# Sliding-window ALiBi attention in front of a gated feed-forward layer: q and k by head pair, a score table added on TensorE, and batch 1 inside the first group

## The chip, the cores and the metric

The kernel runs on one core of one Trainium2 chip. The metric is the device time of one launch in microseconds (us). Five engines work side by side and wait for each other by semaphores: TensorE (PE in the profile; its weight loads are PEld), VectorE (DVE), ScalarE (ACT), GpSimd (POOL) and SyncE (SP). Each runs its own instructions in order. Data lie in HBM, in SBUF (128 partitions) and, for what TensorE writes, in PSUM, which has eight banks of 128 partitions x 512 float32. 16 DMA engines carry the transfers, which SP, ACT and POOL issue.

## The reference

Eight batches of eight heads, 576 tokens, head size 64. Each token attends to itself and the 127 before it; ALiBi subtracts a slope times the distance. The attention output (4608 tokens x 512) goes through two matrices with a gate between them.

```python
scores = scale * np.matmul(q, k.transpose(0, 1, 3, 2))        # q, k, v: 8 x 8 x 576 x 64, float32
rel = pos[:, None] - pos[None, :]
slopes = 2.0 ** (-8.0 * (np.arange(H) + 1) / H)
bias = slopes[:, None, None] * (-np.abs(rel))[None, :, :]
mask = (rel >= 0) & (rel < 128)
scores = np.where(mask, scores + bias[None], -1e9)
attn = softmax(scores)                                        # written out in the reference
x = np.matmul(attn, v).transpose(0, 2, 1, 3).reshape(4608, 512)
h = x @ w_in                                                  # 512 x 2048
g = h * (1.0 / (1.0 + np.exp(-beta * h)))                     # beta: 2048
out = g @ w_out                                               # 2048 x 512
```

## The kernel before

All matrix work is in bfloat16. A batch has five token blocks (`sb`, `kb`, `qb`: four of 128 rows, one of 64) and four head pairs `p`. The steps are these; the names are those of the code and of the profile.

- `load_qk` and `load_v` (L91, L101): SP loads a block of all heads, 128 tokens x 8 heads x 64, in pieces of 256 B (one token of one head), into a float32 tile `fst` (16 buffers), and POOL casts it to bfloat16: q and k into `bst` (L96, L97), v into `vs` (L104), which has a column of ones for the softmax sum.
- `T(b, sb)` (L165): eight TensorE transposes of 128 x 128 into one PSUM tile `tps`, and one VectorE copy into `qkT` (L176), which holds q and k with the head size on the partitions.
- `SC(b, m, p)` (L184): the scores of one head pair, transposed (keys on partitions), for key blocks 0 and 1 (`m` = 0, four matmuls) or 2, 4 and 3 (`m` = 1, six matmuls), into one tile `sps` of two banks, of which there is one buffer. Four ScalarE `Exp` (L207) write `pt`; their `bias` is slope x (key position - a constant), so that ALiBi's query part drops out in the softmax. VectorE multiplies `pt` by a 0/1 mask (L211). The masks are built on POOL before the loop (L120).
- `PV(b, qb, g)` (L219): for four heads, four or eight matmuls with `pt` as weights into `pv`, then reciprocal and product on VectorE into `xn` (L238, L239).
- `X(b, qb)` (L244): four transposes of `xn` and a VectorE copy into `XT` (L254), the feed-forward input with features on partitions.
- `HS(g, j)` (L261): for token group `g` (nine of 512) and one of 16 blocks of the hidden size, four matmuls into `hps` (two banks), ScalarE `Tanh` into `sig` (L272), VectorE `(sig + 1) * hps` into `gT` (L273). Half the gate's argument and the factor 0.5 at the end turn `Tanh` into the sigmoid.
- `OS(g, i, n)` (L277): four of the 16 matmuls that make 128 output rows in `ops` (two banks); after the fourth quarter ScalarE scales them (L289) and SP stores them (L291).

`tps`, `pv` and `xt` share two PSUM buffers (`psum_t`). TensorE's order is written out by hand. A list `att` holds the attention steps of all batches, with `T` and `SC` of one half of a batch merged with `PV` and `X` of the half before. First as much of `att` runs as group 0 needs. Then, in group `g`, 16 `HS(g, j)` alternate with the 16 `OS(g - 1, ...)` and the share of `att` that the next group needs is spread between them; group 0 has only `HS`, and group 1 has its 16 `OS` two by two in its second half. Loads are issued from inside `att` half a batch ahead (`loads_ahead`, L335); the four quarters of W1 are queued on POOL behind the fourth V cast of batch 0 and those of W2 behind a V cast of batch 1.

Of the kernel before, what the change touches and what calls it, by code (L numbers as in the profile page):

```python
# [18 lines left out]
def kernel(  # L19
# [17 lines left out]
    NP = H // 2  # L37
    NQB = 5
# [10 lines left out]
    REF = 63.5  # L49

    const = ctx.enter_context(tc.tile_pool(name="const", bufs=1))
    ident = const.tile([P, P], BF16, name="ident")
    identf = const.tile([NFF, NFF], F32, name="identf")
    bflat = const.tile([NFF, P], F32, name="bflat")
    beta_h = const.tile([P, NFF], F32, name="beta_h")
    one = const.tile([P, 1], BF16, name="one")
    masks = [const.tile([P, 2, 512], BF16, name=f"mask{m}") for m in range(2)]
# [3 lines left out]
    QK = [const.tile([P, 2, NP, NQB * P], BF16, name=f"qkT{i}") for i in range(2)]  # L61
    XT = const.tile([P, NDM, XTR], BF16, name="XT")
# [4 lines left out]
    fst_pool = ctx.enter_context(tc.tile_pool(name="fst", bufs=16))  # L67
    bst_pool = ctx.enter_context(tc.tile_pool(name="bst", bufs=4))
    pt_pool = ctx.enter_context(tc.tile_pool(name="ptp", bufs=11))
    xn_pool = ctx.enter_context(tc.tile_pool(name="xn", bufs=2))  # L70
# [3 lines left out]
    psum_h = ctx.enter_context(tc.tile_pool(name="psum_h", bufs=2, space=bass.MemoryType.PSUM))  # L74
    psum_o = ctx.enter_context(tc.tile_pool(name="psum_o", bufs=2, space=bass.MemoryType.PSUM))
# [4 lines left out]
    def load_rows(src, b, sb):  # L80
        rows = ROWS[sb]
        f = fst_pool.tile([P, H, D], F32, name="fst", tag="fst")
        nc.sync.dma_start(  # L83
            out=f[0:rows],
            in_=src[b, :, P * sb : P * sb + rows, :].rearrange("h p d -> p h d"),
        )
        return f

    staged = {}

    def load_qk(b, sb):  # L91
        rows = ROWS[sb]
        fq = load_rows(q, b, sb)
        fk = load_rows(k, b, sb)
        t = bst_pool.tile([P, 2, H, D], BF16, name="bst", tag="bst")
        nc.gpsimd.tensor_copy(out=t[0:rows, 0], in_=fq[0:rows])  # L96
        c = nc.gpsimd.tensor_copy(out=t[0:rows, 1], in_=fk[0:rows])  # L97
        staged[b, sb] = t
        return c

    def load_v(b, sb):  # L101
        rows = ROWS[sb]
        f = load_rows(v, b, sb)
        return nc.gpsimd.tensor_copy(out=VS[b % 2][0:rows, sb, :, 0:D], in_=f[0:rows])  # L104

    make_identity(nc, ident[:])
    nc.sync.dma_start(out=bflat[:], in_=moe_beta.rearrange("(j p) -> j p", p=P))
    make_identity(nc, identf[:])
    nc.vector.memset(one[:], 1.0)
# [3 lines left out]
    )  # L113

    low = dict(compare_op=ALU.is_ge, fill=0.0, base=0, channel_multiplier=-1)
    up = dict(compare_op=ALU.is_ge, fill=0.0, base=-1, channel_multiplier=1)

    def fill(m, at, n, w, sign, how):
        for e in range(2):
            nc.gpsimd.affine_select(  # L120
                out=masks[m][:, e, at : at + n * w].rearrange("p (n w) -> p n w", w=w),
                in_=bass.AP(tensor=one.tensor, offset=one[:].offset,
                            ap=[list(one[:].ap[0]), [0, n], [0, w]]),
                pattern=[[0, n], [sign, w]], **how,
            )


    fill(0, 0, 2, P, 1, low)
    fill(0, 256, 2, P, -1, up)

    fill(1, 0, 1, P, 1, low)
    fill(1, 128, 1, 64, 1, low)
    fill(1, 192, 1, P, 1, low)
    fill(1, 320, 1, 64, -1, up)
    fill(1, 384, 1, P, -1, up)
    for h in range(H):
        for half in range(2):
            nc.vector.tensor_scalar(
                out=bias[:, half, h : h + 1], in0=kpos[:], scalar1=-(REF + half * P),
                scalar2=slopes[h], op0=ALU.add, op1=ALU.mult,  # L140
            )
    for i in range(2):
        nc.vector.memset(VS[i][64:P, 4, :, :], 0.0)
        nc.vector.memset(VS[i][:, :, :, D : D + 1], 1.0)
        nc.vector.memset(QK[i][:, :, :, S:], 0.0)
    for sb in range(3):
        load_qk(0, sb)

# [9 lines left out]
    bps = psum_t.tile([P, NFF], F32, name="bps", tag="t")  # L158
    nc.tensor.transpose(out=bps[:], in_=bflat[:], identity=identf[:])
    nc.vector.tensor_scalar_mul(beta_h[:], bps[:], 0.5)  # L160
# [4 lines left out]
    def T(b, sb):  # L165
        rows = ROWS[sb]
        src = staged.pop((b, sb))
        tps = psum_t.tile([P, 2, NP, P], BF16, name="tps", tag="t")
        for i in range(2):
            for p in range(NP):  # L170
                nc.tensor.transpose(  # L171
                    out=tps[:, i, p, :],
                    in_=src[:, i, 2 * p : 2 * p + 2, :].rearrange("r h d -> r (h d)"),
                    identity=ident[:],
                )
        nc.vector.tensor_copy(  # L176
            out=QK[b % 2][:, :, :, P * sb : P * sb + rows], in_=tps[:, :, :, 0:rows]
        )

# [4 lines left out]
    def SC(b, m, p):  # L184
        qk = QK[b % 2]
        sps = psum_s.tile([P, 2, 512], F32, name="sps", tag="sps")
        for kb in ((0, 1), (2, 4, 3))[m]:
            at, after = COLS[kb]
            nq = {3: P + 64, 4: 64}.get(kb, 2 * P)
            for e in range(2):  # L190
                o = sps[:, e, at : at + min(nq, 512 - at)]
                if kb in (0, 2):
# [8 lines left out]
                    start=True, stop=True, skip_group_check=True,  # L201
                )
        pt = pt_pool.tile([P, 2, 512], BF16, name="pt", tag="pt")
        for e in range(2):
            h = 2 * p + e
            for half, cols in ((0, slice(0, OWN[m])), (1, slice(OWN[m], 512))):
                nc.scalar.activation(  # L207
                    out=pt[:, e, cols], in_=sps[:, e, cols], func=ACTF.Exp,
                    scale=qscale, bias=bias[:, half, h : h + 1],
                )  # L210
        nc.vector.tensor_tensor(out=pt[:], in0=pt[:], in1=masks[m][:], op=ALU.mult)  # L211
# [7 lines left out]
    def PV(b, qb, g):  # L219
# [19 lines left out]
        nc.vector.tensor_tensor(  # L239
# [4 lines left out]
    def X(b, qb):  # L244
# [9 lines left out]
        nc.vector.tensor_copy(out=XT[:, :, tok0 : tok0 + n1], in_=xt[:, :, 0:n1])  # L254
# [6 lines left out]
    def HS(g, j):  # L261
# [3 lines left out]
        hps = psum_h.tile([P, TOKG], F32, name="hps", tag="hps")  # L265
# [28 lines left out]
    def pvx(b, qbs):  # L294
        r = []
        for qb in qbs:
            r += [(None, lambda g=g, qb=qb: PV(b, qb, g)) for g in range(2)]
            if qb != qbs[0]:
                r.append(((b, qb - 1), lambda qb=qb: X(b, qb - 1)))
        r.append(((b, qbs[-1]), lambda: X(b, qbs[-1])))  # L300
        return r

# [10 lines left out]


    att, before = [], []
    for b in range(B):
        for m in range(2):
            a = [(None, lambda b=b, sb=sb: T(b, sb)) for sb in ((0, 1, 2), (3, 4))[m]]
            a += [(None, lambda b=b, m=m, p=p: SC(b, m, p)) for p in range(NP)]
            att.append((None, lambda b=b, m=m: loads_ahead(b, m)))  # L320
            att += merged(a, before)
            before = pvx(b, ((0, 1), (2, 3, 4))[m])
            if b == 0 and m == 1:
                att += before[:6]
                before = before[6:]
# [3 lines left out]
    def place_of(tok):  # L329
        b, s = divmod(tok - 1, S)  # L330
        return place[b, s // P]
# [3 lines left out]
    def loads_ahead(b, m):  # L335
        if m == 0:
            if b:
                for sb in (3, 4):
                    load_qk(b, sb)
                for sb in (2, 3, 4):  # L340
                    load_v(b, sb)
        elif b + 1 < B:
            for sb in range(3):
                load_qk(b + 1, sb)
            for sb in range(2):
                c = load_v(b + 1, sb)
            if b == 0:
                with tc.issue_after(c.ins):
                    for n in range(4):
                        load_w2(n)  # L350

    with tc.manual_schedule(engines={mybir.EngineType.PE}):
        for sb in range(2):
            load_v(0, sb)
        for sb in (3, 4):
            load_qk(0, sb)
        for sb in (2, 3, 4):
            c = load_v(0, sb)
            if sb == 3:
                with tc.issue_after(c.ins):  # L360
                    for n in range(4):
                        load_w1(n)
        done = 0
        while done < need[0]:
            att[done][1]()
            done += 1
        for g in range(NTG):
            items = []
            for j in range(NFF):
                items.append(lambda g=g, j=j: HS(g, j))  # L370

                lag = [2 * j - NFF, 2 * j - NFF + 1] if g == 1 else [j] if g else []
                items += [lambda g=g, n=n: OS(g - 1, n // 4, n % 4) for n in lag if n >= 0]
            target = need[g + 1] if g + 1 < NTG else len(att)
            start, span_ = done, len(items) - 3
            for n, it in enumerate(items):
                it()
                while done < min(target, start + (target - start) * (n + 1) // span_):
                    att[done][1]()
                    done += 1  # L380
# [32 lines left out]
```

The softmax here doesn't subtract the row's maximum and nothing guards it: scores larger than these inputs give would overflow.

## Time and profile before

| | |
|---|---|
| device time, median of 3 runs | 374.97 us (373.36 to 377.29) |
| the profiled execution's own time | 376.31 us |
| its span, first to last instruction | 374.6 us |
| TensorE matmul busy | 338.5 us, 90% |
| VectorE busy | 224.2 us, 60% |
| ScalarE busy | 214.4 us, 57% |
| POOL busy | 84.4 us, 23% |
| moved by DMA | 42.40 MB, mean 113 GB/s |

Durations come from one execution, by the hardware profiler; the span runs from its first to its last instruction. Busy time of TensorE counts a matmul from its issue to a modelled end, so that matmuls in a row overlap: four of 512 columns that start every 0.216 us are shown as one piece of 1.03 us. In a line of the timeline, x4 is the number of instructions in the piece, and the bracket gives the idle time of the engine ahead of it and the instruction that ended it. In a group's line the numbers behind the first bar are the busy us and the mean ns of one, those behind the second the idle time just before them and what ended most of it.

### The profile page before, as it was taken

The numbers are of one execution on the slowest core, as the hardware profiler recorded it, in microseconds if no ns is written. First come the engines' busy times: TensorE is split into PE (matmuls) and PEld (weight loads), VectorE is DVE, ScalarE is ACT, GpSimd is POOL, SyncE is SP. The second block draws the span as 40 slices with busy tenths as digits, with TensorE's granted clock in tenths as the row PEclk, the third lists the DMA queues.
The fourth block names the chain that finished last, engine by engine and source line by source line (L and its number), as shares of the span: only waits on it lengthen the run. The fifth ranks groups of instructions, "written<-read, shape, count | busy, mean of one in ns | idle before, by whom it ended". The sixth has DMA issues, their size and how long they took to land.

```text
span 374.6 us, 6713 instructions
## 1 busy us (share of the span) xinstructions
PE 338.5 (90%) x2529; PEld 172.7 (46%) x2529; DVE 224.2 (60%) x473; ACT 214.4 (57%) x437; POOL 84.4 (23%) x151
## 2 busy tenths in 40 slices
PE   2367687788999999999999999999999999999995
PEld 1145334434454455445454545454545445544442
DVE  3266467777665677665666776776767755533400
ACT  1453359375745875585846694668566854445421
POOL 7570703453122213112033303320100000000000
PEclk9999999899999999999999999999999999999999
DMA  9999999999297898954138440000000010001012
GB/s 166 209 206 202 193 195 214 192 216 180 76 214 159 159 186 170 205 126 107 50 96 187 109 104 31 28 30 29 30 28 30 30 57 29 29 29 58 28 56 86
DMA packets 121985, 42.40 MB, mean 113 GB/s; under 512 B 113232, under 2 KB 117344, under 8 KB 121952
## 3 DMA queue, kind: packets, MB, share of 16 engines
q1 hardware_dynamic: 117728, 37.77, 47.9%
q0 software_dynamic: 4224, 4.19, 6.7%
q8 instruction: 20, 0.33, 0.4%
q14 instruction: 13, 0.11, 0.1%
HBM read 36.71 MB, written 9.44 MB: 123 GB/s over the span
## 4 chain that ended last, share of the span: by engine, by line
PE 80%; DMA 6%; DVE 4%; ACT 4%; SPq 4%; issue 1%; POOL 0%; ACTq 0%
PE ops L283 34%; PE hps L267 32%; PE sps L197 4%; DMA fst<-in_k_dram 4%; PE tps L171 4%; SPq L83 4%; ACT pt L207 3%; PE xt L249 2%; PE pv L233 2%; DVE gT L273 2%; PE pv L229 2%; DMA fst<-in_v_dram 1%; ACT sig L272 1%; DVE pt L211 1%; DVE qkT L176 1%
## 5 line engine op out<-in xcount | busy, mean ns | idle before, releaser
L272 ACT ACTIVATE sig<-hps,beta_h 128x512 bf16<-128x512 f32 x144 | 99.5, 692 | 98.4 <-PE hps L267 87.4
L267 PE MATMUL hps<-XT,W 128*128 128x512 bf16 x576 | 150.7, 385 | 3.6 <-DVE gT L273 3.0
L283 PE MATMUL ops<-W,gT 128*128 128x512 bf16 x576 | 144.9, 379 | 0.0
L273 DVE SCALAR_TENSOR_TENSOR gT<-sig,hps 128x512 bf16<-128x512 bf16 x144 | 98.3, 683 | 53.0 <-ACT sig L272 52.4
L207 ACT ACTIVATE pt<-sps,bias 128x256 bf16<-128x256 f32 (+2 forms) x256 | 100.4, 480 | 34.9 <-PE sps L197 34.6
L267 PEld LDWEIGHTS <-W 128*128 128x128 bf16 x576 | 51.1, 98 | 56.5 <-issue 10.9
L283 PEld LDWEIGHTS <-gT 128*128 128x128 bf16 x576 | 51.3, 98 | 52.2 <-issue 1.7
L211 DVE TENSOR_TENSOR pt<-pt,mask 128x1024 bf16<-128x1024 bf16 x64 | 46.1, 720 | 21.2 <-ACT pt L207 20.0
L96 POOL CAST bst<-fst 128x512 bf16<-128x512 f32 (+1 forms) x40 | 24.6, 615 | 108.8 <-issue 78.7
L197 PE MATMUL sps<-qkT 64*128 64x256 bf16 (+2 forms) x320 | 28.3, 271 | 14.1 <-ACT pt L207 13.1
L104 POOL CAST vs<-fst 128x512 bf16<-128x512 f32 (+1 forms) x40 | 26.1, 659 | 65.0 <-PE pv L233 38.1
L176 DVE COPY qkT<-tps 128x1024 bf16<-128x1024 bf16 (+1 forms) x40 | 25.5, 637 | 21.5 <-PE tps L171 21.3
L171 PE MATMUL tps<-ident,bst 128*128 128x128 bf16 x320 | 28.8, 240 | 7.8 <-POOL bst L96 4.3
L239 DVE TENSOR_TENSOR xn<-pv,zs 128x256 bf16<-128x256 f32 (+1 forms) x80 | 33.7, 422 | 2.6
L289 ACT ACTIVATE osb<-ops 128x512 f32<-128x512 f32 x36 | 21.6, 601 | 20.8 <-PE ops L283 20.8
L233 PE MATMUL pv<-vs,pt 128*128 128x65 bf16 x320 | 31.0, 200 | 2.5 <-DVE xn L239 1.5
L171 PEld LDWEIGHTS <-bst 128*128 128x128 bf16 x320 | 23.5, 107 | 17.3 <-POOL bst L96 4.9
L197 PEld LDWEIGHTS <-qkT 64*128 64x128 bf16 x320 | 12.4, 97 | 38.2 <-issue 35.1
L233 PEld LDWEIGHTS <-pt 128*128 128x128 bf16 x320 | 23.6, 102 | 13.7 <-issue 1.8
L97 POOL CAST bst<-fst 128x512 bf16<-128x512 f32 (+1 forms) x40 | 25.3, 634 | 9.3 <-DMA fst<-in_k_dram 9.2
L229 PE MATMUL pv<-vs,pt 128*128 128x65 bf16 x256 | 25.8, 200 | 1.8 <-DVE qkT L176 1.2
L229 PEld LDWEIGHTS <-pt 128*128 128x128 bf16 x256 | 21.3, 102 | 8.3 <-DVE xn L239 1.3
(26 smaller groups left out, 74.3 us busy)
## 6 DMA issues: line engine op xcount, KB each, us to landing
out_dram<-osb SPq DMA_DIRECT2D x36, 256.0 KB, 2.0
fst<-in_q_dram SPq DMA_DIRECT2D x32, 256.0 KB, 4.8
fst<-in_k_dram SPq DMA_DIRECT2D x32, 256.0 KB, 4.8
fst<-in_v_dram SPq DMA_DIRECT2D x32, 256.0 KB, 5.0
W<-in_moe_w_in_dram POOLq DMA_DIRECT2D x4, 512.0 KB, 11.5
W<-in_moe_w_out_dram POOLq DMA_DIRECT2D x4, 512.0 KB, 12.6
fst<-in_q_dram SPq DMA_DIRECT2D x8, 128.0 KB, 4.2
fst<-in_k_dram SPq DMA_DIRECT2D x8, 128.0 KB, 4.2
```

The lines of the kernel that those rows point to most:

```text
L171: nc.tensor.transpose(out=tps[:, i, p, :], in_=src[:, i, 2 * p : 2 * p + 2, :].rearrange("r h d -> r (h d)"), identity=ident[:],)
L176: nc.vector.tensor_copy(out=QK[b % 2][:, :, :, P * sb : P * sb + rows], in_=tps[:, :, :, 0:rows])
L197: nc.tensor.matmul(o, lhsT=qk[64 * e : 64 * e + 64, 1, p, P * kb : P * kb + P], rhs=qk[64 * e : 64 * e + 64, 0, p, P * kb : P * kb + nq], ...
L207: nc.scalar.activation(out=pt[:, e, cols], in_=sps[:, e, cols], func=ACTF.Exp, scale=qscale, bias=bias[:, half, h : h + 1],)
L211: nc.vector.tensor_tensor(out=pt[:], in0=pt[:], in1=masks[m][:], op=ALU.mult)
L229: nc.tensor.matmul(pv[:, hl, 0 : D + 1], lhsT=weights(b, qb - 1, h, 1), rhs=vs[:, qb - 1, h, 0 : D + 1], start=True, stop=False,)
L233: nc.tensor.matmul(pv[:, hl, 0 : D + 1], lhsT=weights(b, qb, h, 0), rhs=vs[:, qb, h, 0 : D + 1], start=qb == 0, stop=True,)
L239: nc.vector.tensor_tensor(out=xn[0:nq, 4 * g : 4 * g + 4, :], in0=pv[0:nq, :, 0:D], in1=zs[0:nq].broadcast_to([nq, 4, D]), op=ALU.mult,)
L267: nc.tensor.matmul(hps[:], lhsT=W1[:, c, bass.ts(j, P)], rhs=XT[:, c, c0 : c0 + TOKG], start=(c == 0), stop=(c == NDM - 1),)
L272: nc.scalar.activation(out=sig[:], in_=hps[:], func=ACTF.Tanh, scale=beta_h[:, j : j + 1])
L273: nc.vector.scalar_tensor_tensor(out=gts[g][:, j, :], in0=sig[:], scalar=1.0, in1=hps[:], op0=ALU.add, op1=ALU.mult)
L283: nc.tensor.matmul(ops_[:], lhsT=gT[:, j, i * P : i * P + P], rhs=W2[:, j, :], start=(j == 0), stop=(j == NFF - 1),)
```

## The change

- `load_qk(b, p)` now loads one head pair: partition `r` gets tokens 4r to 4r + 3 of both heads (512 tokens), so a piece in HBM is four tokens of one head, 1 KB. POOL's cast reorders to (token in four, head, feature). The last 64 tokens of all heads come in two more loads with the first pair, into `tails`. `T(b, p, i)` makes five transposes (four of the 128 rows, one of the tail) for q or k of one pair, and two VectorE copies; the first interleaves the four.
- In batches 0 and 1 (`NPE` = 2) two matmuls per `SC` first put a table into `sps`: a diagonal matrix of slope / scale times a 128 x 512 table of key position - constant, with -1e12 where the mask is 0. The score matmuls add to it, one `Exp` covers all 1024 columns, and neither bias nor mask product follows. From batch 2 on bias and mask are as before, with the mask held once for both heads of a pair. The table comes from an iota on POOL and about 20 VectorE instructions; mask and bias tiles are made after batch 0's attention.
- All of batch 0's attention now runs ahead of group 0, its `SC` with two more `sps` buffers in the four banks that `hps` and `ops` get afterwards. `XT` of batch 0 is copied by ScalarE.
- Group 0 has `hps` on four banks (the `ops` banks too), and batch 1's `T` and `SC` come in four lumps after each four `HS`; its `PV` and `X` (but for the last `X`) follow the 16th. Group 1 runs its 16 `HS` first and its 16 `OS` after them, with `att` from the ninth `HS` on. From batch 2 on the halves of a batch are head pairs 0, 1 and 2, 3, and `PV` of a half goes over all five blocks.
- All loads of batch 1 are issued at the start, behind those of batch 0. `bflat` is issued by ScalarE. Pools: `fst` 7, `fqk` 8, `bst` 8, `xn` 6 buffers.

```diff
+    def load_qk(b, p):
+        for i, src in enumerate((q, k)):
+            f = fqk_pool.tile([P, 2, LA, D], F32, name="fqk", tag="fqk")
+            nc.sync.dma_start(
+                out=f[:].rearrange("r h a d -> r h (a d)"),
+                in_=src[b, 2 * p : 2 * p + 2, 0:LM].rearrange("h (r a) d -> r h (a d)", a=LA),
+            )
+            t = bst_pool.tile([P, LA, 2, D], BF16, name="bst", tag="bst")
+            nc.gpsimd.tensor_copy(out=t[:], in_=f[:].rearrange("r h a d -> r a h d"))
+            staged[b, p, i] = t
+        if p == 0:
...
+                nc.gpsimd.tensor_copy(out=tails[b % 2][0 : S - LM, i], in_=f[0 : S - LM])
...
+    def T(b, p, i):
+        src = staged.pop((b, p, i))
+        tps = psum_t.tile([P, LA + 1, P], BF16, name="tps", tag="t")
+        for a in range(LA):
+            nc.tensor.transpose(
+                out=tps[:, a, :], in_=src[:, a, :, :].rearrange("r h d -> r (h d)"),
+                identity=ident[:],
+            )
...
+        nc.vector.tensor_copy(
+            out=to[:, 0:LM].rearrange("c (r a) -> c r a", a=LA),
+            in_=tps[:, 0:LA, :].rearrange("c a r -> c r a"),
+        )
+        nc.vector.tensor_copy(out=to[:, LM:S], in_=tps[:, LA, 0 : S - LM])
...
-    def SC(b, m, p):
+    def SC(b, m, p, pool=None):
         qk = QK[b % 2]
-        sps = psum_s.tile([P, 2, 512], F32, name="sps", tag="sps")
+        sps = (pool or psum_s).tile([P, 2, 512], F32, name="sps", tag="sps")
+        if b < NPE:
+            for e in range(2):
+                nc.tensor.matmul(
+                    sps[:, e, :], lhsT=sident[:, 2 * p + e, :], rhs=table[m][:],
+                    start=True, stop=False, skip_group_check=True,
+                )
...
-                    start=True, stop=True, skip_group_check=True,
+                    start=b >= NPE, stop=True, skip_group_check=True,
...
+        if b < NPE:
+            nc.scalar.activation(out=pt[:], in_=sps[:], func=ACTF.Exp, scale=qscale)
+        else:
...
-        nc.vector.tensor_copy(out=XT[:, :, tok0 : tok0 + n1], in_=xt[:, :, 0:n1])
+        copy = nc.vector.tensor_copy if b else nc.scalar.copy
+        copy(out=XT[:, :, tok0 : tok0 + n1], in_=xt[:, :, 0:n1])
...
-        hps = psum_h.tile([P, TOKG], F32, name="hps", tag="hps")
+        pool, tag = (psum_o, "ops") if g == 0 and j % 2 else (psum_h, "hps")
+        hps = pool.tile([P, TOKG], F32, name="hps", tag=tag)
...
+    for b in range(1, B):
+        for half in range(2):
+            a = []
+            for p in (2 * half, 2 * half + 1):
+                a += [(None, lambda b=b, p=p, i=i: T(b, p, i)) for i in range(2)]
+                if p % 2 and b > 1:
+                    a += [(None, lambda b=b, p=p, m=m: SC(b, m, p - 1)) for m in range(2)]
+                if p % 2 or b == 1:
+                    a += [(None, lambda b=b, p=p, m=m: SC(b, m, p)) for m in range(2)]
+            if b > 1 or half:
+                att.append((None, lambda b=b, half=half: loads_ahead(b, half)))
+            att += merged(a, before)
...
+        with tc.tile_pool(name="psum_x", bufs=2, space=bass.MemoryType.PSUM) as psum_x:
+            nsc = 0
+            for p in range(NP + 1):
+                if p < NP:
+                    for i in range(2):
+                        T(0, p, i)
+                if p:
+                    for m in range(2):
+                        SC(0, m, p - 1, psum_s if nsc % 3 == 2 else psum_x)
+                        nsc += 1
...
+        for qb in range(NQB):
+            for g in range(2):
+                c = PV(0, qb, g)
+            if qb:
+                X(0, qb - 1)
+        X(0, NQB - 1)
+        with tc.issue_after(c.ins):
+            late_consts()
...
-                lag = [2 * j - NFF, 2 * j - NFF + 1] if g == 1 else [j] if g else []
-                items += [lambda g=g, n=n: OS(g - 1, n // 4, n % 4) for n in lag if n >= 0]
+                if g > 1:
+                    items.append(lambda g=g, j=j: OS(g - 1, j // 4, j % 4))
+            if g == 1:
+                items += [lambda j=j: OS(0, j // 4, j % 4) for j in range(NFF)]
             target = need[g + 1] if g + 1 < NTG else len(att)
-            start, span_ = done, len(items) - 3
+            lead = 8 if g == 1 else 0
+            start, span_ = done, len(items) - 3 - lead
             for n, it in enumerate(items):
                 it()
-                while done < min(target, start + (target - start) * (n + 1) // span_):
+                to = start + (target - start) * (n + 1 - lead) // span_
+                if g == 0:
+
+                    to = NB1 * ((n + 1) // 4) // 4 if n + 1 < NFF else target
+                while done < min(target, to):
                     att[done][1]()
                     done += 1
```

## The prediction

> **What bounds the kernel now.** I read the page's 40 slices first, then TensorE's timeline of the first 95 us, then the groups by line with shapes kept apart, then the waits.
>
> ```profile
> PE   2367687788999999999999999999999999999995
> DMA  9999999999297898954138440000000010001012
> ```
>
> From slice 11 on (94 us) TensorE is busy without a break; before that it is not, and the DMA engines are. To see what a full TensorE is worth I priced its work by its own timeline: four `hps` or `ops` matmuls take 0.864 us from start to start (groups in a row start at 224.46, 225.32, 226.19), the `sps` group of one `SC` 0.33, a 128-column transpose 0.056, a `pv` matmul 0.031, the four of `X` 0.225. The first `ops` matmul starts at 93.71. In the compiled order 119 `hps` groups, 144 `ops` groups, 44 `SC`, 200 transposes of `T`, 424 `pv` matmuls and 30 `X` follow: 272.8 us. They end at 370.8, 277.1 us later: only 4.3 us are lost there. Ahead of 93.71 stand 41.9 us of the same work, so 52 us are lost, all in the first quarter. What waits are they?
>
> ```profile
> 14.83 0.61 PE L197 MATMUL sps<-qkT 64*128 64x256 bf16 x4 [1.66 <-ACT pt L207]
> ...
> 42.44 1.87 PE L267 MATMUL hps<-XT,W 128*128 128x512 bf16 x4 [0.52 <-DVE XT L254]
> ...
> 80.19 1.89 PE L267 MATMUL hps<-XT,W 128*128 128x512 bf16 x8 [0.73 <-DVE gT L273]
> ```
>
> The columns are start, length, engine, line, and in brackets the idle time ahead with what ended it. The first line: one `sps` tile, so the next `SC` waits for four `Exp`. The second: the first `hps` starts at 42.44, and its four matmuls run at half pace. The third: `hps` groups in a row, on two banks, wait for `Tanh` and `gT`; two of them then cost 2.52 us (80.19 to 82.71) and not 1.73.
>
> ```profile
> L272 ACT ACTIVATE sig<-hps,beta_h 128x512 bf16<-128x512 f32 x144 | 99.5, 692 | 98.4 <-PE hps L267 87.4 <-DVE xn L239 10.2 <-DVE gT L273 0.3
> L273 DVE SCALAR_TENSOR_TENSOR gT<-sig,hps 128x512 bf16<-128x512 bf16 x144 | 98.3, 683 | 53.0 <-ACT sig L272 52.4
> L207 ACT ACTIVATE pt<-sps,bias 128x256 bf16<-128x256 f32 x128 | 50.2, 478 | 26.8 <-PE sps L197 26.6
> L239 DVE TENSOR_TENSOR xn<-pv,zs 128x256 bf16<-128x256 f32 x64 | 27.1, 424 | 2.1
> L176 DVE COPY qkT<-tps 128x1024 bf16<-128x1024 bf16 x32 | 22.1, 690 | 19.6 <-PE tps L171 19.5
> L176 DVE COPY qkT<-tps 128x512 bf16<-128x512 bf16 x8 | 3.4, 424 | 1.9 <-PE tps L171 1.8
> ```
>
> Here the second number after the bar is the mean ns of one. They price the new operations below.
>
> So the end is: start of the first `ops` matmul + work left on TensorE + stalls + 3.8 us (last `osb` and its store, 370.8 to 374.6). In the changed order 32 `hps` groups, not 25, and four `SC` of batch 2 stand ahead of the first `ops`; 267.5 us of priced work stand behind it. The change draws level if its first `ops` starts at 93.71 + 272.8 - 267.5 = 99.0 with no new stall behind it.
>
> **Part A, loads and batch 0, up to the first `hps`.** A 256 KB load in 256 B pieces takes 1.2 us (the casts that wait for one follow at 7.11, 8.31, 9.53). A 1 KB piece is not in this trace. Bounds: 1.2 us, and 0.68 us, since the 2 KB rows of the stores move 27 GB/s at a DMA share of 0.07 (240 to 260 us). By time per piece (18.7 and 85 ns) 1 KB lies at 47 ns: I take 0.75 us. SP issues its first load at about 0.85 and not 1.26, as `bflat` goes to ScalarE's queue; data flow from about 3.1. Eight loads of 0.75 and two tails of 0.6 land by 10.3, five loads of V by 15.7 (W1, queued on POOL behind the fourth V cast, is issued at 16 and not 20.46; its chunks took 11.5 us to land). POOL's 3.75 us of mask building go; about 3 us of iota and memsets take their place and end as q lands. VectorE's table building (about 20 instructions of 0.1 to 0.2 us) ends near 6, as the first transposes do. Both are hidden by the loads.
>
> The exponential over 1024 columns is new too. `Exp` of 256 costs 478 ns, the 512 columns of `Tanh` 692: 0.84 ns a column, hence 1.1 us, against four in 1.57. Ends: 1.0 and 1.57. Eight of them behind the first `sps` (about 10 us) and behind TensorE at half pace give the last at 20.6; the 16 table matmuls lie in this wait. Then `PV` and `X` alternate on two `psum_t` buffers: 15 tiles. One `pv` tile costs TensorE 0.44 at half pace and 0.2 drain, VectorE 0.63 (0.21 to the `xn`, 0.42 of it); two buffers make 0.69 a tile, 10.4 us, from 19.0 on. `X` copied by ScalarE (0.69) fits the same step. First `hps`: **29.3**, 13 us earlier; 27 if TensorE runs at full pace, 32 if the loads stay at 1.2.
>
> **Part B, group 0 with batch 1 in it.** The order puts four `hps`, then `T`, `T`, `SC`, `SC` of one pair, with nothing in between. A block at full pace: 3.46 for `hps` (four banks, no wait), 0.56 for ten transposes, 0.43 for the first table matmuls. The copies stand on VectorE behind three `gT` and with a fourth between them. A copy that reads 512 columns in four interleaved runs is not in the trace: 0.42 as the contiguous form, or 0.69 at the 1.03 ns a column that `gT` and `xn` pay. `xn` also reads in pieces and is nearest: 0.69, and 0.19 for the tail copy. Then `SC` can start at 6.4, its `Exp` ends at 8.0, and the second `SC`, on the one `sps` tile, at 8.8. First block 11 (half pace at its start), second 8.9. The third ends after its first `SC` at 6.7; four `hps` (10.2), the second `SC`, `T`, `T` and the two `SC` of the last pair follow by 15.8, and then 10 `PV` tiles and four `X` alone, 8.3 us plus the copy: 24.3. Sum 44.2 for 25.2 us of work; group 1 starts at **73.5** (before: 81.05). Ends: 38 with copies of 0.42 and no half pace, 48 with half pace after each wait.
>
> A rule bears on the copy. The Trainium skill, "VectorE: DVE Perf Modes", section "What auto-detection actually checks", ties the packed rate of 16-bit data to a step of one element in every tensor. The interleaved read steps 128, so the page says 0.69 and speaks against this part; without it each block would be some 0.5 us shorter. The second is on pace: `hps` at 42.44 took 1.87 and at 93.71 1.02. "TensorE: Matmul & The Clock Gate", section "What's actually happening", gives half rate after an idle window of some 3.4 us; by it the waits of 2.0 and 1.3 us in a block keep full pace.
>
> **Part C, group 1 up to `ops`.** Nine `hps` in a row at 1.265 are 11.4 us. Three more with 25 transposes and `X` reach 15.4. Then four `SC` stand between four `hps`: ScalarE needs 1.57 + 0.6 for each pair, and the one `sps` tile makes TensorE follow: 9.2. With 1.3 for half pace after the `PV` stretch: 25.9, and the first `ops` at **99.4**. Ends 22 and 28. For a check, the pace of before from its first `hps` to its first `ops` (32.2 us of work in 51.3) makes 42.4 us of work 67.5: 96.8.
>
> **Part D, behind it.** Before, two `SC` never stand closer than two `hps`/`ops` groups there. In the changed order nine pairs have one group between them (three in group 1, six later). From `SC` to `SC` the single tile needs 0.45 + 1.57 + 0.05 and up to 0.6 for a `Tanh` ahead; TensorE has 1.19 to 1.44 us to do. Stall 0.6 to 1.5, I take 0.95: 8.5 us. The eight copies of a batch cost VectorE 7.0 us and not 3.2; it was busy 14 us in 20 and goes to 16, hidden while `gT` keeps within its 1.7 us of slack (an `hps` returns to its bank after 4.2 us, its chain takes 2.5); without cover each late `gT` is a TensorE stall. The mask read twice from one tile keeps 0.72, at most 1.2; `PV` comes three groups later. Loads keep their number and have half a batch, 20 us, of lead; smaller pools cost nothing.
>
> **Sum.** 99.4 + 267.5 + 4.3 + 8.5 + 3.8 = 383.5; with 96.8, 380.9. I take 382 against a span of 374.6 (that execution took 376.3; the median shown is 375.0, 0.4 above the span, inside its spread).
>
> **Rivals.** *Slower, 378.7 to 391* (0.50): the sum; against it, that it adds up many waits, any of which may overlap. *Faster, about 369* (0.24): group 0 packs better than 44. It decides there: ScalarE has 18.4 us of work in group 0 (16 x 0.6, 8 x 1.1) and TensorE 25.2, so no engine forces 44. At 80% of TensorE group 0 takes 31.5, and the end is 369 to 370; level with before at 37, faster by over 1% below 33. Against: queues run in order. *No change, 371.2 to 378.7* (0.22): the short `SC` gaps cost nothing, since `Exp` may start earlier: 382 - 8.5 = 373.5. *Far slower, 392 or more* (0.04): late `gT`, 0.2 us for each of 112, +22; VectorE's reserve speaks against it. That the loads do not speed up costs 3 us and lies inside the first.
>
> The bounds of the terms give 366.7 (27 + 38 + 22, short gaps at half) to 395; 367 to 392 holds eight in ten, the likeliest alone 379 to 391. About 1% is what a measurement here tells from no change: faster 0.24, within 0.22, slower 0.54.
>
> **What would show it.** First `hps` at 27 to 32; group 1 at 68 to 77; first `ops` at 95 to 101; qkT copies of 0.69 and `Exp` of 1.1; TensorE waiting for `pt` 0.6 to 1.5 us about nine times behind 100 us. A group 0 under 37 us, or no such stalls, makes it wrong.

## The result: 3.8% slower

| | before | after |
|---|---|---|
| device time, median of 4 runs | 375.76 us (373.36 to 377.29) | 389.75 us (388.17 to 391.25) |
| ratio to before, 95% interval | | 1.0378 (1.030 to 1.0455) |
| span of the profiled execution | 374.6 us | 388.7 us |
| first `hps` matmul | 42.44 us | 28.68 us |
| first `hps` of group 1 | 81.05 us | 74.51 us |
| first `ops` matmul | 93.71 us | 102.76 us |

The slices of the changed kernel's page, 9.7 us each (busy tenths of TensorE, and the clock that it was granted):

```profile
PE   2987787886879998999999989998999899999996
PEclk9968897599899999999999999999999999999999
```

Two things differ from before. The broken stretch reaches to the end of slice 12 (117 us) and not of slice 10 (94 us), and in it the granted clock falls in slices 3, 4, 5, 7, 8 and 11. Behind it slices 16, 24, 28 and 32 are an 8, where before all were 9. The clock row, and every mean clock below, counts the time ahead of a trace's first clock record as full pace. That record comes at 12.5 us in the changed kernel. In the kernel before it comes at 50.5 us, and the matmuls up to there show half pace (four `hps` matmuls took 1.87 us at 42.44 and 1.89 at 47.08).

The groups by line, with shapes kept apart, hold the new operations (the second number behind the bar is the mean ns of one):

```profile
L198 DVE COPY qkT<-tps 128x512 bf16<-128x512 bf16 x64 | 43.9, 686 | 11.7 <-PE tps L192 11.3
L202 DVE COPY qkT<-tps 128x64 bf16<-128x64 bf16 x64 | 11.7, 183 | 0.0
L235 ACT ACTIVATE pt<-sps 128x1024 bf16<-128x1024 f32 x16 | 16.0, 1026 | 22.9 <-PE sps L227 22.8
L240 ACT ACTIVATE pt<-sps,bias 128x256 bf16<-128x256 f32 x96 | 37.7, 480 | 7.7 <-PE sps L227 7.4
```

The interleaved copy costs 0.69 us where 512 contiguous columns cost 0.42, and one `Exp` over 1024 columns 1.03 us where four took 1.57. Now TensorE's own timeline, a line of each kind of wait:

```profile
36.94 0.39 PE L227 MATMUL sps<-qkT 64*128 64x256 bf16 x4 [1.54 <-DVE qkT L198]
38.45 0.59 PE L213 MATMUL sps<-table,sident 128*128 128x512 bf16 x2 [1.12 <-ACT pt L235]
...
48.46 4.40 PE L306 MATMUL hps<-XT,W 128*128 128x512 bf16 x16
...
79.29 2.13 PE L306 MATMUL hps<-XT,W 128*128 128x512 bf16 x8 [0.39 <-DVE gT L312]
...
188.06 0.40 PE L227 MATMUL sps<-qkT 64*128 64x256 bf16 x6 [0.69 <-ACT pt L240]
...
226.56 0.40 PE L227 MATMUL sps<-qkT 64*128 64x256 bf16 x6 [0.94 <-ACT pt L240]
...
265.93 0.40 PE L227 MATMUL sps<-qkT 64*128 64x256 bf16 x6 [0.95 <-ACT pt L240]
...
307.15 0.40 PE L227 MATMUL sps<-qkT 64*128 64x256 bf16 x6 [1.07 <-ACT pt L240]
```

The first two are one lump of group 0: `SC` waits for the copies of the `T` just ahead of it, and the second `SC` for the `Exp` of the first. At 48.46 sixteen `hps` matmuls take 4.40 us where 3.63 is the full pace (sixteen at 55.72). At 79.29 groups of `hps` in a row wait for `gT`. The last four are short gaps between `SC`, from four batches. The waits of TensorE from 102.7 us to the end (us in all, times, longest; the kernel before has no such wait behind its first `ops`):

```profile
PE sps L227 <- ACT pt L240: 6.8, 9, 1.1
```

**Where the 14.1 us of span come from.** The first `ops` comes 9.05 us later, but with 5.3 us more of priced work done (272.8 less 267.5): 3.8 us are lost ahead of it. From there to the last `osb` 282.2 us pass for 267.5 of work, 14.7 lost; before, 277.2 for 272.8, 4.4 lost. So 10.3 us come behind the first `ops`. The 3.8 us ahead of it are a difference: the first `hps` comes 13.8 us earlier than before, and groups 0 and 1 lose that again and more.

### The profile page after: what moved, and what is told of

Read it like the earlier page. It is cut to its first block, busy times and chain, and to the rows that moved or that the text cites. A ratio compares the mean times of both kernels' runs of the same rounds, so it can differ in the third digit from the quotient of the medians.

```text
span 388.7 us, 6816 instructions
## 1 busy us (share of the span) xinstructions
PE 346.2 (89%) x2515; PEld 174.1 (45%) x2561; DVE 240.9 (62%) x560; ACT 209.9 (54%) x394; POOL 82.5 (21%) x140
## 4 chain that ended last, share of the span: by engine, by line
PE 76%; ACT 10%; DVE 9%; issue 2%; POOL 1%; POOLq 0%; ACTq 0%
PE hps L306 29%; PE ops L322 29%; ACT pt L240 5%; PE sps L227 5%; PE tps L188 3%; ACT sig L311 3%; DVE gT L312 3%; PE xt L286 3%; PE pv L270 2%; DVE qkT L198 2%; PE pv L266 2%; PE sps L213 2%; DVE xn L276 2%; ACT pt L235 1%; PE tps L192 1%
## 5 line engine op out<-in xcount | busy, mean ns | idle before, releaser
L322 PE MATMUL ops<-W,gT 128*128 128x512 bf16 x556 | 141.9, 379 | 1.4 <-issue 0.6
L240 ACT ACTIVATE pt<-sps,bias 128x256 bf16<-128x256 f32 (+1 forms) x192 | 75.3, 479 | 11.8 <-PE sps L227 11.6
L322 PEld LDWEIGHTS <-gT 128*128 128x128 bf16 x576 | 50.8, 98 | 50.5 <-issue 3.0
L97 POOL CAST bst<-fqk 128x512 bf16<-128x512 f32 x64 | 39.0, 618 | 101.8 <-issue 62.0
L198 DVE COPY qkT<-tps 128x512 bf16<-128x512 bf16 x64 | 43.9, 686 | 11.7 <-PE tps L192 11.3
L244 DVE TENSOR_TENSOR pt<-pt,mask 128x1024 bf16<-128x1024 bf16 x48 | 34.2, 712 | 12.6 <-ACT pt L240 12.4
L188 PE MATMUL tps<-ident,bst 128*128 128x128 bf16 x256 | 25.2, 226 | 8.3 <-POOL bst L97 5.2
L275 DVE RECIPROCAL zs<-pv 128x4 f32<-128x4 f32 (+1 forms) x80 | 14.3, 178 | 23.2 <-PE pv L270 20.9
L235 ACT ACTIVATE pt<-sps 128x1024 bf16<-128x1024 f32 x16 | 16.0, 1026 | 22.9 <-PE sps L227 22.8
L188 PEld LDWEIGHTS <-bst 128*128 128x128 bf16 x256 | 18.9, 100 | 20.9 <-POOL bst L97 8.7
L270 PEld LDWEIGHTS <-pt 128*128 128x128 bf16 x320 | 23.9, 103 | 8.8 <-issue 0.8
## 6 DMA issues: line engine op xcount, KB each, us to landing
W<-in_moe_w_in_dram POOLq DMA_DIRECT2D x4, 512.0 KB, 14.7
W<-in_moe_w_out_dram POOLq DMA_DIRECT2D x4, 512.0 KB, 12.8
```

The costliest lines, as they stand in the source:

```text
L97: nc.gpsimd.tensor_copy(out=t[:], in_=f[:].rearrange("r h a d -> r a h d"))
L188: nc.tensor.transpose(out=tps[:, a, :], in_=src[:, a, :, :].rearrange("r h d -> r (h d)"), identity=ident[:],)
L198: nc.vector.tensor_copy(out=to[:, 0:LM].rearrange("c (r a) -> c r a", a=LA), in_=tps[:, 0:LA, :].rearrange("c a r -> c r a"),)
L240: nc.scalar.activation(out=pt[:, e, cols], in_=sps[:, e, cols], func=ACTF.Exp, scale=qscale, bias=bias[:, half, h : h + 1],)
L270: nc.tensor.matmul(pv[:, hl, 0 : D + 1], lhsT=weights(b, qb, h, 0), rhs=vs[:, qb, h, 0 : D + 1], start=qb == 0, stop=True,)
L322: nc.tensor.matmul(ops_[:], lhsT=gT[:, j, i * P : i * P + P], rhs=W2[:, j, :], start=(j == 0), stop=(j == NFF - 1),)
```

## The experiments

Theory A: TensorE's order makes it wait, in the lumps of group 0 and in nine short gaps between `SC`. Theory B: the interleaved copies burden VectorE, and the waits follow. Theory C: the 32 table matmuls cost their time. Ratios are to the kernel before, run on the same chip.

### Two groups between SC

```diff
-            att += merged(a, before)
+            if b > 1 and half:
+                tq, tk, uq, uk, s0, s1, s2, s3 = a[0], a[1], a[2], a[3], *a[4:]
+                v0, v1, v2, v3, v4 = before
+                att += [tq, tk, uq, s0, v0, uk, s1, v1, v2, s2, v3, v4, s3]
+            else:
+                att += merged(a, before)
```

> From batch 2 on, the second half of each batch is ordered by hand so that two SC always have at least two hps or ops groups between them; nothing else changes. Theory A (TensorE waits that the new order makes): the changed kernel's trace has nine pairs of SC with one group between them behind the first ops, each with some 0.9 us of waiting (0.75 us idle and the drain); this order takes away eight of them, so 7 us: a span near 381.5 and a ratio to the kernel before near 1.018. Theory B (VectorE: the interleaved qkT copies of 0.69 us make everything late): no change, ratio 1.038. Theory C (the 32 table matmuls cost their 6.9 us of TensorE): no change.

Measured: 381.76 us, ratio 1.0179 (1.0108 to 1.025), span 380.6: 8.1 us less, as theory A had it (forecast 7). Of the 6.8 us that TensorE waited for `pt` behind 103 us, 0.2 us are left:

```profile
PE sps L227 <- ACT pt L240: 0.2, 1, 0.2
```

B and C fall for this part: copies and table are untouched.

### The copy in order

```diff
-            out=to[:, 0:LM].rearrange("c (r a) -> c r a", a=LA),
-            in_=tps[:, 0:LA, :].rearrange("c a r -> c r a"),
+            out=to[:, 0:LM].rearrange("c (a r) -> c a r", a=LA),
+            in_=tps[:, 0:LA, :],
```

> The qkT copy reads its four runs one after the other and not interleaved; left out is the reordering of tokens, so the scores belong to permuted tokens. The copy should take 0.42 us and not 0.69: 64 x 0.27 = 17 us less VectorE. Theory A: only copies that TensorE waits for count, two in each of four blocks of group 0 and a few behind: 2 to 4 us, a span near 386, ratio 1.028. Theory B: most of the 14 us goes, ratio 1.00 to 1.01. Theory C: no change.

The same group of VectorE in this run, 0.27 us less for one:

```profile
L198 DVE COPY qkT<-tps 128x512 bf16<-128x512 bf16 x64 | 26.9, 420 | 15.8 <-PE tps L192 15.3
```

Measured: three runs of 386.7 to 387.3 us at a mean granted clock of 0.965, and one of 380.9 at 0.995, so no ratio is given. The changed kernel at a clock of 0.96 took 390.8 and 391.3: at like clocks the copies are worth 3.5 to 4 us of the 17 that VectorE spends less, as theory A had it. The run at 0.995 is 8.8 us under the changed kernel's median; that kernel has no run at such a clock beside it, so how much of this is the copies stays open. No run came to theory B's 1.00 to 1.01 (375 to 379 us). The spread by clock is a finding of its own (below).

### Group 0 spread evenly

```diff
-                if g == 0:
-
-                    to = NB1 * ((n + 1) // 4) // 4 if n + 1 < NFF else target
```

> Batch 1's T, SC, PV and X are spread evenly between the 16 hps groups of group 0, not in four lumps and a tail. Theory A: group 0, 45.8 us from its first hps to that of group 1, has 25.2 us of TensorE work and falls to some 37; a span near 380, ratio 1.014. Theories B and C: group 0 keeps its length within 2 us.

Measured: 378.27 us, ratio 1.0097 (1.0068 to 1.0125), span 375.6, mean granted clock 0.998 and not 0.960. The first `hps` is at 29.5, that of group 1 at 63.7: 34.2 us, not 45.8. The first `ops` comes at 89.83. The slices:

```profile
PE   1977689777799989999999899989999899999995
PEclk9999999999999999999999999999999999999999
```

The lumps cost 11.5 us, more than the 9 of theory A. Waits and half pace go together here; this run does not part them.

### The table in batch 0 only

```diff
-    NPE = 2
+    NPE = 1
```

> Batch 1 takes its ALiBi bias and mask as the later batches do (four Exp with bias, mask product), only batch 0 keeps the table. Theory C: 16 table matmuls of 0.216 us less, the span falls by 3.5 us to 385. Theory A: the table matmuls of the first SC of a pair lie in the wait for the copies, those of the second cost 0.43, and against it the Exp of one tile takes 1.57 us and not 1.03 while the next SC waits: no gain, a span of 388 to 393, ratio 1.036 to 1.05.

Measured: 392.84 us, ratio 1.048 (1.0424 to 1.0537), the upper part of theory A's range. Theory C falls for batch 1: 3.5 us of table matmuls less, and the median is 3 us up and not down (the intervals of the two kernels overlap). The 16 table matmuls of batch 0 were not taken out in any run.

### Both orders together

The edits of the first and the third experiment in one kernel.

> The two orders together: group 0 spread evenly, and two groups between SC from batch 2 on. If the two losses are separate stretches of TensorE's queue they add: 390 less 8 and less 11.5, about 370, ratio 0.985 to 0.99. If one only uncovers the other (VectorE or the loads then end last), 375 to 378, ratio 1.00 to 1.01.

Measured: 370.12 us, ratio 0.9881 (0.9826 to 0.9936). The two gains add: 389.75 less 8.0 and less 11.5 is 370.3. This kernel has the packing, the table and the early head, and is faster than the one before.

### And group 1 as before

```diff
-                if g > 1:
-                    items.append(lambda g=g, j=j: OS(g - 1, j // 4, j % 4))
-            if g == 1:
-                items += [lambda j=j: OS(0, j // 4, j % 4) for j in range(NFF)]
+                lag = [2 * j - NFF, 2 * j - NFF + 1] if g == 1 else [j] if g else []
+                items += [lambda g=g, n=n: OS(g - 1, n // 4, n % 4) for n in lag if n >= 0]
...
-            lead = 8 if g == 1 else 0
+            lead = 0
```

> The same, and group 1 ordered as in the kernel before: its ops two by two in the second half and the attention steps from its first hps on. In the run with group 0 spread, ten hps in a row wait 0.63 us for gT at each second one, some 3.5 us, and the SC there 3 us. If that is waiting that other work can fill: 366 to 368, ratio 0.98. If the loads of batch 2 are late or the SC between hps wait as much: no change against the run with both orders.

Measured: 365.76 us, ratio 0.976 (0.9714 to 0.9806), 4.4 us less than with both orders. The `hps` in a row cost what the prediction's part C said (2.52 us for two, 79.29 to 81.81 in the changed kernel), and other work can fill it.

### The packing undone, in the changed kernel

```diff
-            nc.sync.dma_start(
-                out=f[:].rearrange("r h a d -> r h (a d)"),
-                in_=src[b, 2 * p : 2 * p + 2, 0:LM].rearrange("h (r a) d -> r h (a d)", a=LA),
-            )
+            for e in range(2):
+                nc.sync.dma_start(
+                    out=f[:, e],
+                    in_=src[b, 2 * p + e, 0:LM].rearrange("(a r) d -> r a d", a=LA),
+                )
...
-            out=to[:, 0:LM].rearrange("c (r a) -> c r a", a=LA),
-            in_=tps[:, 0:LA, :].rearrange("c a r -> c r a"),
+            out=to[:, 0:LM].rearrange("c (a r) -> c a r", a=LA),
+            in_=tps[:, 0:LA, :],
```

> Only the packing undone in the changed kernel: q and k of a pair come in pieces of 256 B (a load for each head), the token blocks lie one after the other and the qkT copy is in order. Theory A (order): the first hps starts some 3 us later than 28.7, as eight loads take 1.2 and not 0.75 us each, and the shorter copies give back some 3: a span of 386 to 391, ratio 1.03 to 1.045. If the packing is what makes the first quarter possible (a rival for why the head is early): first hps at 35 or later, ratio 1.055 or more. If the interleaved copies were the loss: below 1.02.

Measured: median 384.87 us; the four runs took 381.8, 382.9, 386.8 and 387.7 us at mean granted clocks of 0.996, 0.987, 0.973 and 0.965. The ratio, of the first three, is 1.0237 (1.0155 to 1.0319). The first `hps` is at 29.53, only 0.85 us later than with 1 KB pieces in the changed kernel; among the other runs with 1 KB pieces it lies between 27.9 and 29.7. So the packing is not what brings the head forward (the rival's 35 us or later did not come), and it was no gain here. Which of the head's other parts does (the table, the extra `sps` buffers, the order) no run takes apart. The ratio lies just under theory A's range, and its interval reaches both that and the 1.02 and below of B: this run does not decide between them.

### Short gaps put into the kernel before

```diff
-            att += merged(a, before)
+            mix = merged(a, before)
+            if b > 1 and m == 1:
+                ts, ss = a[:2], a[2:]
+                v0, v1, v2, v3, x0, x1 = before[0], before[1], before[2], before[3], before[4], before[5]
+                mix = [ts[0], v0, ts[1], v1, ss[0], ss[1], v2, v3, ss[2], ss[3], x0, x1]
+            att += mix
```

> The kernel before, with one thing of the change: in the second half of each batch from the third on, SC stand in pairs with one group between them. That makes eight or nine short gaps behind the first ops where there was none. Theory A: each waits about 0.9 us, 7 to 8 us, a span near 382, ratio 1.02. Theory B (waiting there is an effect of VectorE's load by the interleaved copies, which this kernel has not): ratio below 1.008.

Measured: 384.82 us, ratio 1.025 (1.0192 to 1.0309), 10 us slower. Its waits of TensorE from 94 us on:

```profile
PE sps L197 <- ACT pt L207: 7.8, 9, 0.9
```

Nine waits, 7.8 us of idle time, and with the drain that the profile counts as busy (some 0.16 us each) 9.2. This kernel has neither interleaved copies nor a table: the spacing of `SC` on one `sps` tile is the cause by itself.

### More work for TensorE in the waits

```diff
-            for e in range(2):
+            for e in range(2) if b == 0 or m else (0, 1, 0, 1, 0, 1):
...
+    def fill():
+        sps = psum_s.tile([P, 2, 512], F32, name="sps", tag="sps")
+        nc.tensor.matmul(
+            sps[:, 0, :], lhsT=sident[:, 0, :], rhs=table[0][:], start=True, stop=True
+        )
...
+        if b == 0 or b == 1 and qb:
+            fill()
```

> The changed kernel with more work for TensorE, none of it used: one 512-column table matmul into an unread sps tile behind each PV and X of batches 0 and 1 (28 of them), and the table matmuls of the first SC of each pair of batch 1 three times over (16 more). Everything else, the lumps and short gaps too, stays. Question: how much of the loss in the lumps is waiting, and how much that TensorE runs at half pace after it (in the changed kernel the granted clock was 0.65 from 20 to 29 us, 0.75 from 47 to 53, 0.50 from 64 to 75). If half pace costs by itself, the filler keeps the mean clock near 1.00 and the span falls from 388.7 to 382 to 385, though 44 matmuls (9.5 us of work, nearly all in waits) are added. If only the waits count: no change or up to 4 us slower.

The stretches of both kernels, the changed one and then this run: window, then busy time and count of PE, PEld, DVE, ACT and POOL, granted clock, DMA share, GB/s.

```profile
20.00:29.00 9.00, 7.47 (x89) 5.10 (x88) 6.57 (x33) 3.28 (x6) 6.25 (x11) 0.65 1.17 258
...
47.00:53.00 6.00, 6.00 (x30) 2.42 (x30) 1.63 (x3) 3.20 (x5) 2.99 (x6) 0.75 1.21 198
...
64.00:75.00 11.00, 9.06 (x97) 6.19 (x97) 7.18 (x24) 1.02 (x1) 5.95 (x11) 0.50 1.09 231
```

```profile
20.00:29.00 9.00, 8.89 (x109) 5.10 (x108) 6.86 (x38) 3.42 (x7) 6.23 (x11) 1.00 1.16 257
...
47.00:53.00 6.00, 6.00 (x30) 2.66 (x28) 2.57 (x4) 3.47 (x5) 3.02 (x6) 0.73 1.22 197
...
64.00:75.00 11.00, 9.06 (x112) 5.24 (x110) 7.74 (x26) 2.40 (x3) 6.34 (x11) 1.00 1.05 248
```

Measured: 387.44 us, ratio 1.0332 (1.0277 to 1.0387), span 385.4. The trace has 27 matmuls behind `PV` and `X`, so 43 more in all. Where the filler stands behind `PV` and `X` the clock stays at 1.00; the lumps it did not hold (0.73). The span is 3.3 us shorter with 43 matmuls more, but the medians differ by 2.3 us with overlapping intervals: less than expected, and only a sign. Group 1 starts at 72.16 and not 74.51. The `PV` stretches show it best, from their first `pv` to the `hps` behind them: 8.3 us and not 9.1 in batch 0 (19.62 to 27.88; 19.55 to 28.68), 8.1 and not 9.4 in batch 1 (64.02 to 72.16; 65.11 to 74.51), with 15 and 12 matmuls more in them. So half pace by itself costs some 2 us in the two stretches; the 8 us that are left of each are not due to it.

### The packing undone, with the three orders mended

The two edits of the packing in the kernel with group 0, group 1 and the short gaps mended.

> The run with all three orders mended (group 0, short gaps, group 1) and the packing undone: 256 B pieces, blocks in order, contiguous qkT copy. Without lumps and half pace in the way this shows what the packing itself is worth. If the earlier landing counts (first hps 1 to 3 us later here): 367 to 369, ratio 0.98 to 0.985. If the copies of 0.69 us cost as much as the landing gives: 364 to 367, ratio 0.972 to 0.979.

Measured: 367.03 us, ratio 0.9791 (0.9743 to 0.9839), beside 0.976 (0.9714 to 0.9806) with the packing, on another chip. The intervals overlap (the medians are 1.3 us apart): the packing's faster landing and slower copies come out even, as far as these runs tell.

### The table in batch 0 only, with the three orders mended

> The same run with the table in batch 0 only; batch 1 with bias and mask. The table matmuls of batch 1 are 3.5 us of TensorE, and group 0 has waits for pt and qkT to hold some of them. If the table pays in batch 1 through the short Exp (1.03 and not 1.57 us, no mask product): slower by 2 to 4 us, ratio 0.982 to 0.987. If not: faster by 1 to 3, ratio 0.968 to 0.973.

The edit is again `NPE` = 1. Measured: 373.51 us, ratio 0.9975 (0.995 to 1.0001): 7.7 us slower than with the table in both batches, twice the expectation. The stretch where it comes about, in the same columns as above:

```profile
20.00:40.00 20.00, 12.76 (x146) 7.53 (x141) 13.32 (x52) 9.38 (x19) 7.97 (x14) 0.87 1.16 230
40.00:60.00 20.00, 15.25 (x96) 7.14 (x95) 11.64 (x24) 13.05 (x30) 9.48 (x14) 0.62 1.17 209
```

With the table in both batches (the kernel with the three orders mended) the same stretch keeps its clock:

```profile
20.00:40.00 20.00, 14.16 (x157) 7.92 (x157) 11.85 (x50) 9.93 (x15) 7.90 (x15) 1.00 1.15 227
40.00:60.00 20.00, 16.62 (x167) 8.92 (x169) 13.94 (x37) 11.30 (x15) 8.64 (x14) 1.00 1.19 219
```

So the table gains more than the shorter `Exp`: from 20 to 60 us TensorE also keeps its pace. From 28 to 100 us TensorE waits 12.8 us for `pt` and `qkT` ahead of an `SC` without batch 1's table and 8.2 with it. How the 7.7 us divide between waits and pace was not tried.

### Groups 0 and 1 ordered by hand

Batch 1's steps, and batch 2's first `SC`, in place of the merged lists:

```diff
+    att = [
+        t_(1, 0, 0), t_(1, 0, 1), t_(1, 1, 0), s_(1, 0, 0), t_(1, 1, 1), s_(1, 0, 1),
+        l_(1, 1), t_(1, 2, 0), s_(1, 1, 0), t_(1, 2, 1), s_(1, 1, 1), t_(1, 3, 0),
+        s_(1, 2, 0), t_(1, 3, 1), s_(1, 2, 1), v_(1, 0, 0), s_(1, 3, 0), v_(1, 1, 0),
+        v_(1, 2, 0), s_(1, 3, 1), v_(1, 3, 0), v_(1, 0, 1), v_(1, 1, 1), x_(1, 0),
...
+            if b == 2 and not half:
+                att += [a[0], a[1], a[2], a[4], a[3], a[5]]
+                late = a[6:]
```

Here `t_`, `s_`, `v_`, `x_` and `l_` are `T`, `SC`, `PV`, `X` and the loads; `a` holds four `T` and four `SC`.

> The run with all three orders mended, and the T, SC and PV of batch 1 and the first SC of batch 2 ordered by hand, so that in groups 0 and 1 too no SC stands next to the T it needs or to another SC. There TensorE still waits some 8 us for pt and qkT in groups 0 and 1. If these waits are the order's: 360 to 363, ratio 0.96 to 0.969. If ScalarE or VectorE then bound groups 0 and 1: 364 to 366, ratio 0.972 to 0.977.

Measured: **358.17 us, ratio 0.9571 (0.953 to 0.9613)**, 4.3% faster than the kernel before and better than expected. The slices of its page:

```profile
PE   1988998899999999999999999999999999999995
PEclk9999999999999999999999999999999999999999
```

TensorE's waits for `pt` and `qkT` ahead of an `SC`, 8.2 us in groups 0 and 1 of the kernel that it started from, are gone. The first `ops` comes at 70.34. What is left ahead of it is mainly the wait for the first loads and the `PV` stretch of batch 0.

## Why the prediction was right in its direction and short in its size

The sign and the mechanism held; the forecast of 382, 1.9% slower, was just under half of the 3.8% measured. What failed is the size of two terms, part C (25.9 us, measured 28.25) and the loss behind the first `ops` that was carried over from before (4.3 us, measured 6.4), and a check on pace that took 1.5 us off the sum; part B was 1.6 us short. By its steps:

- **Part A** held: first `hps` at 28.68, forecast 29.3. Its sentence that the pieces matter (3 us later with slow loads) was too strong: with 256 B pieces the first `hps` is at 29.53. In both kernels the casts of q and k end well before the matmuls of the last `SC` start (11.95 and 19.06 us; 15.05 and 19.91), and a `PV` stretch of 9.1 us follows.
- **Part B** held: 45.8 us, forecast 44.2; the copy 0.69, taken at 0.69; `Exp` 1.03, taken at 1.1. TensorE waited 1.5 us for the copies and 1.1 for `Exp` in each of the first two lumps, less than the 2.0 and 1.3 forecast, and half pace at 47 us, which had no term, took that back: in part the good fit is luck. The `PV` stretch took 9.4 us and not 8.5.
- **Part C** was mis-sized: 28.25 us, forecast 25.9, and the first `ops` at 102.76 lies outside the 95 to 101 that it gave as a sign. The nine `hps` with half pace at their start took 11.8 us (forecast 11.4 + 1.3). Too short were the three `hps` with `X` and transposes (5.1 us, forecast 4.0), the four `SC` with four `hps` (10.2, forecast 9.2) and what stands between the last `hps` and the first `ops` (1.2, no term). Half pace stands there a second time, at 100 us behind the 1.66 us wait of the last `SC` (four `hps` matmuls in 1.60 us), and transposes waited for the copies of the ones ahead (0.43, 0.66 us), which had no term:

```profile
97.56 0.40 PE L227 MATMUL sps<-qkT 64*128 64x256 bf16 x6 [1.66 <-ACT pt L240]
...
100.10 1.60 PE L306 MATMUL hps<-XT,W 128*128 128x512 bf16 x4
...
102.48 0.38 PE L188 MATMUL tps<-ident,bst 128*128 128x128 bf16 x4 [0.66 <-DVE qkT L202]
```

- **Part D** held in kind: nine waits for `pt`, 6.8 us idle and 8.3 with the drain, forecast 8.5. The rest of the loss behind the first `ops` was taken over from before, 4.3 us; it was 6.4. The trace shows single waits of 0.2 to 1.0 us for copies and `xn` there, 2.3 us in all, that the kernel before does not have.
- **The sum** of the parts, 383.5, fell 5.2 us short of the span of 388.7 (-0.6, +1.6, +2.4, +1.9). Two choices made it worse. The pace check (96.8 for the first `ops`, which came at 102.76) took 1.5 us off; it assumed that waits of the new order are no denser than those of the old. And the time of a run was put at most 0.4 us above the span; in the profiled run it was 2.1 above, and the median is 1.05 above that span.

The rivals: that group 0 packs better than 44 us was no property of the work but of the order, as its terms said (no engine forces 44): spread evenly it takes 34.2. That short gaps cost nothing fell twice, by taking them away and by putting them in. Late `gT` for every `hps` did not come.

On the two rules. The Trainium skill, "VectorE: DVE Perf Modes", section "What auto-detection actually checks", gives the condition of 16-bit data and a step of one, and no time; the trace agrees with it: 0.69 us for the interleaved copy against 0.42 for the same columns in order. "TensorE: Matmul & The Clock Gate", section "What's actually happening", names an idle window of some 3.4 us. The clock did not do what was read out of that: waits of 1.5 and 1.1 us with some 0.4 us of matmuls between them were enough once for a granted clock of 0.75 from 47 to 53 us, and the same two waits in the lump before were not. Full pace was taken for granted there.

The changed kernel's trace shows more. Behind 12.5 us its clock is at a half from 22.75 to 32.99, 46.65 to 50.05, 63.71 to 77.36 and 97.84 to 101.25 us: each of these stretches is 3.41 us long or a multiple of it, and so are the times between them. In the 3.41 us ahead of the last three TensorE was busy for 1.1, 1.5 and 1.1 us; where it was busy for 1.7 us or more in a step of this grid in the lumps, full pace followed. Ahead of the first it was busy for 2.5 us, nearly all of it with small matmuls. So no single wait has to be long: it fits these stretches that the work in a fixed step of 3.41 us decides, which no run here was made to test.

## What to carry to other kernels

When a change regroups work on an in-order engine, count in the new order how many steps stand between an instruction and the one that frees its buffer, and price each distance shorter than that round trip: nine distances of one group and not two cost 8 us here, and were the same 8 to 10 us in another kernel. Put independent long matmuls between a transpose and its use, between score tiles on one buffer and between small reductions; the same parts that made the kernel 3.8% slower in lumps made it 4.3% faster when spread. A pace measured in an old order is no check on a new one.

## What was not expected of the hardware

The granted clock is a price on waits that a sum of waits leaves out: the changed kernel stood at half pace for 30.7 us behind its first full stretch. In the changed kernel it was 0.65 in the `PV` stretch of batch 0 and 0.50 in that of batch 1, where TensorE has only small matmuls; 27 unread 512-column matmuls there held it at 1.00. One kernel, on one chip, took 380.9 us in a run at a mean clock of 0.995 and 386.7 to 387.3 in three at 0.965; another 381.8 to 387.7 at 0.996 to 0.965. The kernels with the table in both batches and group 0 spread ran at 0.98 to 1.00, and each one's times agreed within 0.9%. Times so far apart in the same code on the same inputs were not in the spread of the kernel before (373.1 to 377.3).
